# Attention and experts on one Trainium2 core: the gate's terms in two products, a gather and a scatter that wait for relus, and waits of PSUM tiles one by one

## The chip, the cores and the metric

One core of one Trainium2 chip. The metric is the device time of one launch in microseconds (us), median of the runs; lower is better. TensorE is PE in the tables, VectorE DVE, ScalarE ACT, GpSimd POOL, SyncE SP.

## The reference, cut to what matters

```
def attention(q, k, v, g_q, g_k):                 # 8 x 12 x 448 x 64
    q_n, k_n = rmsnorm(q, g_q), rmsnorm(k, g_k)
    scores = q_n @ k_n.T / 8
    attn = softmax(scores)
    return attn @ v
x = attention(...).transpose(0, 2, 1, 3).reshape(3584, 768)

logits = x @ w_gate                               # 8 experts
expert_idx = argmax(logits, 1)
gate_w = softmax(logits)[arange(N), expert_idx]
out = zeros(3584, 768)
for e in range(8):
    tok = the (at most 80) tokens of expert e with the largest gate_w
    h = maximum(x[tok] @ w1[e], 0)                # 768 x 1024
    out[tok] = gate_w[tok] * (h @ w2[e])          # 1024 x 768
```

## The kernel before, in words

**Attention.** 24 groups, each a batch and four of its 12 heads (three groups to a batch). For a group, ACT and DVE normalise q and k (L307 to L344), PE transposes them (L381), ACT copies the transposes (L410, L412), PE makes the scores (`ps`, L423), ACT exponentiates them (`at`, L426), DVE sums them over the keys (`sm`, L456, L458) and PE multiplies with v (`po`, L440). The softmax is not divided here: the rows `xb` stay undivided, are copied by ACT (L743) and stored to DRAM (`xr_scratch`) beside the reciprocals `rz` of their sums; a row is divided when an expert takes it up.

**Gate.** Once a batch, PE makes the gate's products per head and the sums (`zl`, L475), which come back transposed as `zs` (the last batch: `zt`). `gate1v` (L510) has two reciprocals of the sums (L516, one for each pair of heads `u`) and four products (L524, one for each head of a group of four), term by reciprocal, into `lx`; `gate2` (L538) reduces `lx` over the 12 heads to the logits `lg` (L541), finds the largest, and ACT exponentiates and casts (L553, L555). Behind this come the merge steps that keep, batch by batch, the best 80 tokens of each expert (`mp`, `row`, L624 to L720). All of it is put between the groups' matmuls in an order written out by hand. The last batch's gate and merge are done apart (L930 to L1146), where `by_head`, `by_block` and `by_half` divide that batch's rows with `rz`, and `xno` the rows gathered as `xo`.

**Experts.** A loop over e = 0 to 7 (L1181). In each turn PE makes `ph` from the transposed rows `xgT` and w1 (L1188, two PSUM tiles of 24 matmuls), ACT casts them through two relus into `h_sb` (L1192), DVE divides the next expert's gathered rows in three pieces of four heads (`normal(e + 1)`, L1157, `xg` into `xn`), PE transposes these (`xpose`, L1172, `pxt`), DVE copies them to `xgT` (L1174), PE multiplies `h_sb` with w2 (`py`, L1219), and DVE weights the product (`yo`, L1224). PE takes these in that order, expert by expert. Rows come in by an indirect DMA on POOL's queue (`gather`, L1119) and go out by another (`scatter`, L1209). The first gather is issued before the loop (L1123); `gather(2)` and `gather(3)` follow it at L1180, so that POOL has three issues in a row; the later ones, `gather(e + 4, wait=True)`, wait for a memset on DVE (L1118) and are issued in the loop. A gather brings 80 rows of 780 floats. The second expert's turn (e = 1) has no `normal` of its own, since `normal(2)` is done at the end of e = 0. The last expert is scattered in two halves (`idxL`), the others whole (`idxT`).

**Weights.** Weights of later experts are staged in DRAM and fetched on SP's queue as buffers come free (`fetch_late`, L242, 1,536 KB each; `fetch_part`, L928, the second part of one w2, which waits for a memset at L927 that `normal(1)` issues behind its first piece).

PSUM tiles of the experts' part come from the pool `moe_ps` (L1150), which takes over the space of the pools that were closed before it.

Of the kernel before, what the change touches and what calls it, by code (L numbers as in the profile page):

```python
# [21 lines left out]
def kernel(  # L22
# [243 lines left out]
    with av_stack:  # L266
# [243 lines left out]
        def gate1v(b):  # L510
            zt = gst[b]["zt"]
            NT = NJ + 1
            ztv = zt.rearrange("p r (j c) -> p r j c", c=64)
            rz = gpool.tile([128, NT, H], F32, tag="rz", name="rz")
            for u in range(2):
                nc.vector.reciprocal(  # L516
                    rz[:].rearrange("p j (i u hh) -> p j u i hh", u=2, hh=2)[:, :, u],
                    ztv[:, 1 - u].rearrange("p j (hh r) -> p j r hh", hh=2)[
                        :, :, 24:24 + NQ])
            lx = gpool.tile([128, NT, E, H], F32, tag="lx", name="lx", bufs=1)  # L520
            for u in range(2):
                for hh in range(2):
                    r = 32 * u
                    nc.vector.tensor_mul(  # L524
                        lx[:].rearrange("p j e (i k) -> p j k i e", k=4)[:, :, 2 * u + hh],
                        ztv[:, hh, :, r:r + NQ * E].rearrange("p j (i e) -> p j i e", e=E),
                        rz[:].rearrange("p j (i k) -> p j k i", k=4)[:, :, 2 * u + hh]
                        .unsqueeze(3).to_broadcast([128, NT, NQ, E]))
            gst[b]["lx"] = lx
            gst[b]["rz"] = rz  # L530
            rows = xr_dram[b * S:(b + 1) * S, DM:XW].rearrange("(p x) h -> p x h", x=NX)
            for t in range(2):
                n = NJ + 1 - t if b < B - 1 else NJ
                nc.sync.dma_start(out=rows[:, t:t + 2 * n - 1:2], in_=rz[64 * t:64 * t + 64, :n])
            if b == B - 1:
                nc.sync.dma_start(out=rows[:, NX - 1], in_=rz[64:, NJ])

        def gate2(b):  # L538
            NT = NJ + 1
            lg = gpool.tile([128, NT, E], F32, tag="lg", name="lg")  # L540
            nc.vector.reduce_sum(out=lg[:], in_=gst[b]["lx"][:], axis=AX.X)  # L541
            lmax = gpool.tile([128, NT], F32, tag="lmax", name="lmax")
# [390 lines left out]
    m, NT = gst[b], NJ + 1  # L933
    xbs, rz = [st[NQ * b + i]["xb"] for i in range(NQ)], m["rz"]
    xbn = [mpool.tile([128, NT, 256], BF16, tag="yo", name="xbn", bufs=3) for _ in range(NQ)]

    def by_head(i, part):
        for n in part:
# [3 lines left out]
                                 xbs[i][:, j, h * D:h * D + D], AF.Copy,  # L942
                                 scale=rz[:, j, 4 * i + h:4 * i + h + 1])

    def by_block(i, j):
        nc.vector.tensor_mul(
            xbn[i][:, j].rearrange("p (hh u d) -> p u hh d", hh=2, u=2),
            xbs[i][:, j].rearrange("p (u hh d) -> p u hh d", u=2, hh=2),
            rz[:, j, 4 * i:4 * i + 4].rearrange("p (u hh) -> p u hh", hh=2)
            .unsqueeze(3).to_broadcast([128, 2, 2, D]))  # L950

    def by_half(i, u, eng=nc.vector):
        eng.tensor_mul(
            xbn[i][:].rearrange("p j (hh u d) -> p u j hh d", hh=2, u=2)[:, u],
            xbs[i][:].rearrange("p j (u hh d) -> p u j hh d", u=2, hh=2)[:, u],
            rz[:, :, 4 * i + 2 * u:4 * i + 2 * u + 2].unsqueeze(3).to_broadcast([128, NT, 2, D]))

# [51 lines left out]
    def rows_normal(i, xn, xg):  # L1009
        c = slice(256 * i, 256 * i + 256)  # L1010
        return (xn[:, c].rearrange("p (hh u d) -> p u hh d", hh=2, u=2),
                xg[:, c].rearrange("p (u hh d) -> p u hh d", hh=2, u=2),
                xg[:, DM + 4 * i:DM + 4 * i + 4].rearrange("p (u hh) -> p u hh", hh=2)
                .unsqueeze(3).to_broadcast([CAP, 2, 2, D]))

    for h in range(4):
        u, hh = divmod(h, 2)
        o = hh * 128 + u * D
        nc.scalar.activation(xno[:, o:o + D], xo[:, h * D:h * D + D], AF.Copy,
                             scale=xo[:, DM + h:DM + h + 1])  # L1020
    stay = tpool.tile([CAP, E], BF16, name="stay")
# [84 lines left out]
    xgs = {}  # L1106
    def gather(e, wait=False):

# [8 lines left out]
        if wait:  # L1117
            nc.vector.memset(xgs[e][:, 0:1], 0.0)  # L1118
        nc.gpsimd.indirect_dma_start(  # L1119
            out=xgs[e], out_offset=None, in_=xr_dram[:, :],  # L1120
# [28 lines left out]
    ps_stack.close()  # L1149
    mps = ctx.enter_context(tc.tile_pool(name="moe_ps", bufs=2, space=PSUM))  # L1150


    def normal(e, behind=None):
        xg = xgs[e]
        xn = mpool.tile([CAP, DM], BF16, tag="xn", name="xn")
        for i in range(NQ):
            nc.vector.tensor_mul(*rows_normal(i, xn, xg))  # L1157
            if behind and not i:
                behind()
        return xn  # L1160
# [17 lines left out]

    for e in range(2, 4):
        gather(e)  # L1180
    for e in range(E):  # L1181
# [12 lines left out]
        if e + 1 < E and e != 1:  # L1194
            xn = normal(e + 1, (lambda: fetch_part(slice(FE, FC), True)) if not e else None)
        if 0 < e < E - 1:
# [5 lines left out]

        def scatter(half=None):
            if half is None:
                o, at, y, n = outs[e], idxT[:, e:e + 1], yo[:, :], N
            else:
# [6 lines left out]
        pw = DN if e + 1 < E else DN // 2  # L1213
        pys = [mps.tile([CAP, pw], F32, tag=("py", "py", "pz", "pxt")[i], name="py",
                        bufs=2 if i < 2 else 1) for i in range(DM // pw)]

# [10 lines left out]
        if e + 1 < E:  # L1227
# [7 lines left out]
            for i in range(2):  # L1235
                weighted(i)
            scatter()
        else:
            for fh in range(2):
                for i in range(2):  # L1240
# [46 lines left out]
```

## Time and profile before

| | |
|---|---|
| median of 3 runs | 409.39 us (408.94 to 409.46) |
| the profiled execution | 408.7 us, its span 407.0 us |
| PE busy | 395.7 us (97%) |
| DVE busy | 352.2 us (87%) |
| ACT busy | 320.6 us (79%) |
| POOL busy | 90.2 us (22%) |
| DMA | 100.92 MB, mean 248 GB/s |
| mean granted TensorE clock | 0.999 of full speed |

The span is the time from the first to the last instruction of the profiled execution; 1.7 us of its 408.7 lie around it. A busy share is an average over stages, so the stretch in question and its waits have to be looked at apart. In a row of the timeline the first number is the start, the second the duration, and the brackets tell how long the engine stood idle before and what ended that.

### The profile page before, as it was taken

The numbers are of one execution on the slowest core, as the hardware profiler recorded it, in microseconds if no ns is written. First come the engines' busy times: TensorE is split into PE (matmuls) and PEld (weight loads), VectorE is DVE, ScalarE is ACT, GpSimd is POOL, SyncE is SP. The second block draws the span as 40 slices with busy tenths as digits, with TensorE's granted clock in tenths as the row PEclk, the third lists the DMA queues.
The fourth block names the chain that finished last, engine by engine and source line by source line (L and its number), as shares of the span: only waits on it lengthen the run. The fifth ranks groups of instructions, "written<-read, shape, count | busy, mean of one in ns | idle before, by whom it ended". The sixth has DMA issues, their size and how long they took to land.

```text
span 407.0 us, 12628 instructions
## 1 busy us (share of the span) xinstructions
PE 395.7 (97%) x5285; PEld 195.4 (48%) x5285; DVE 352.2 (87%) x658; ACT 320.6 (79%) x508; POOL 90.2 (22%) x150
## 2 busy tenths in 40 slices
PE   8999999999999999999999999999999999999994
PEld 7334444444444444444444444444443453458884
DVE  5899987998999999997999999979999968876552
ACT  6899979997989889988899799979897877572110
POOL 7200002501031012220251024020512020154322
PEclk9999999999999999999999999999999999999999
DMA  7459999999989999989999999999999759798991
GB/s 244 144 159 212 272 296 257 273 217 304 254 223 264 246 260 263 294 205 228 243 306 217 243 278 230 289 237 285 219 205 297 161 195 374 245 277 274 342 333 52
DMA packets 76105, 100.92 MB, mean 248 GB/s; under 512 B 8448, under 2 KB 65280, under 8 KB 76048
## 3 DMA queue, kind: packets, MB, share of 16 engines
q1 hardware_dynamic: 60176, 70.99, 54.7%
q0 software_dynamic: 15872, 29.13, 39.3%
q8 instruction: 41, 0.67, 0.6%
q14 instruction: 16, 0.13, 0.1%
HBM read 101.11 MB, written 39.89 MB: 346 GB/s over the span
## 4 chain that ended last, share of the span: by engine, by line
PE 73%; DVE 12%; ACT 8%; issue 5%; POOL 2%; POOLq 0%; DVEq 0%
PE ps L423 26%; PE po L440 25%; PE zl L475 5%; DVE sm L458 4%; PE tp L381 4%; PE xp L381 3%; DVE ms L314 2%; DVE qn L344 2%; PE py L1219 2%; PE wps L894 2%; ACT at L426 1%; PE ph L1188 1%; POOL out_dram L1209 1%; ACT qkT L412 1%; PE mp L666 1%
## 5 line engine op out<-in xcount | busy, mean ns | idle before, releaser
L426 ACT ACTIVATE at<-ps 128x896 f32<-128x896 f32 x168 | 146.5, 930 | 4.5 <-PE ps L423 3.9
L423 PE MATMUL ps<-qkT 64*64 64x448 f32 x1344 | 147.3, 548 | 2.5 <-ACT row L624 1.3
L440 PE MATMUL po<-at,vt 64*64 64x448 f32 x1344 | 142.5, 537 | 0.0
L458 DVE TENSOR_TENSOR sm<-sm,at 128x896 f32<-128x896 f32 x120 | 130.7, 1089 | 3.4 <-ACT at L426 0.5
L440 PEld LDWEIGHTS po<-at,vt 64*64 64x64 f32 x1344 | 50.1, 133 | 74.0 <-issue 63.9
L423 PEld LDWEIGHTS ps<-qkT 64*64 64x64 f32 x1344 | 43.8, 132 | 66.6 <-issue 26.2
L314 DVE TENSOR_REDUCE ms<-sq 128x14 f32<-128x896 f32 (+1 forms) x50 | 52.1, 1043 | 6.9 <-ACT sq L307 6.8
L344 DVE TENSOR_TENSOR qn<-qk,rs 128x896 f32<-128x896 f32 (+1 forms) x47 | 50.5, 1077 | 1.3
L307 ACT ACTIVATE sq<-qk 128x896 f32<-128x896 f32 (+1 forms) x48 | 44.7, 930 | 2.0 <-DMA qk<-in_q_dram 1.1
L229 POOL COPY mark<-mark 1x1 bf16<-1x1 bf16 x22 | 7.8, 354 | 138.0 <-DVE mark L228 138.0
L743 ACT COPY xb<-xp 128x1024 f32<-128x1024 f32 x24 | 24.3, 1011 | 8.4 <-PE xp L381 8.3
L381 PEld LDWEIGHTS tp<-ident,qn 64*128 64x128 f32 x672 | 23.5, 139 | 12.1 <-issue 6.0
L381 PE MATMUL tp<-ident,qn 64*128 64x64 f32 x672 | 27.2, 226 | 0.3 <-DVE qn L344 0.3
L1192 ACT ACTIVATE h_sb<-ph 128x320 bf16<-128x320 f32 x16 | 7.0, 438 | 25.7 <-PE ph L1188 25.7
L447 ACT COPY us<-po 128x896 f32<-128x896 f32 (+1 forms) x24 | 21.4, 894 | 6.5 <-PE po L440 6.4
L456 DVE TENSOR_TENSOR sm<-at 128x896 f32<-128x896 f32 x24 | 26.0, 1084 | 0.1
L412 ACT COPY qkT<-tp 128x896 f32<-128x896 f32 x24 | 22.0, 917 | 3.3 <-PE tp L381 3.1
L410 ACT ACTIVATE qkT<-tp,gqk 128x896 f32<-128x896 f32 x23 | 23.6, 1025 | 0.0
L1219 PE MATMUL py<-w_sb,h_sb 128*80 128x384 bf16 (+1 forms) x144 | 22.4, 309 | 0.0
L475 PE MATMUL zl<-us,wgs 64*32 64x448 f32 x192 | 20.3, 540 | 0.0
L1224 DVE TENSOR_SCALAR yo<-py,gwT 80x384 f32<-80x384 f32 (+1 forms) x18 | 10.0, 568 | 11.7 <-PE py L1219 11.6
L475 PE MATMUL zl<-sm,zsel 64*32 64x448 f32 x192 | 20.1, 541 | 0.0
(202 smaller groups left out, 433.2 us busy)
## 6 DMA issues: line engine op xcount, KB each, us to landing
wb_scratch<-in_moe_w_dram POOLq DMA_DIRECT2D x20, 768.0 KB, 10.5
w_sb<-wb_scratch SPq DMA_DIRECT2D x8, 1536.0 KB, 11.4
vt<-in_v_dram SPq DMA_DIRECT2D x24, 448.0 KB, 7.6
out_dram<-zeros SPq DMA_DIRECT2D x28, 384.0 KB, 10.0
qk<-in_q_dram SPq DMA_DIRECT2D x23, 448.0 KB, 6.5
qk<-in_k_dram SPq DMA_DIRECT2D x23, 448.0 KB, 5.3
w_sb<-in_moe_w_dram POOLq DMA_DIRECT2D x6, 1536.0 KB, 14.9
xr_scratch<-xb SPq DMA_DIRECT2D x48, 192.0 KB, 6.7
```

The source lines that it names most:

```text
L307: nc.scalar.activation(o, x, AF.Square)
L314: nc.vector.reduce_sum(out=st[g]["ms"][:, a, lo:hi], in_=st[g]["sq%d" % a][:, lo:hi], axis=AX.X)
L344: e.tensor_mul(qn[:].rearrange("p (x hh) d -> p hh x d", hh=2)[:, h0:h1], qk[:, lo:hi].rearrange("p (hh x) d -> p hh x d", x=NX), rs[:, lo ...
L381: nc.tensor.transpose(o, w, one[p, p], tile_position=(p.start, 0))
L412: nc.scalar.copy(T[:], tp[:, :, :S])
L423: nc.tensor.matmul(ps[u * 64:u * 64 + 64, hh, :S], T1[d, u, x * 64:(x + 1) * 64], T0[d, u, :], start=True, stop=True)
L426: nc.scalar.activation(at[:], ps[:, :, :S], AF.Exp)
L440: nc.tensor.matmul(po[u][hh * D:(hh + 1) * D, u, :S], vt[p, hh * NX + x, :], at[p, hh, :], start=(x == 0), stop=(x == RD - 1))
L456: nc.vector.tensor_add(s["sm"][:], s["at0"][:], s["at1"][:])
L458: nc.vector.tensor_add(s["sm"][:], s["sm"][:], s["at%d" % x][:])
L475: nc.tensor.matmul(t[32 * c:32 * c + 32, r, :S], w, x, start=(i == 0), stop=(i == NQ - 1))
L1219: nc.tensor.matmul(pys[i][:, :], h_sb[:, fc, :], chunk(e, 1, fc)[:, i * pw:i * pw + pw], start=(fc == 0), stop=(fc == FC - 1))
```

## The change

It has four parts.

1. `gate1v` makes one reciprocal of 48 columns and two products of 192 columns; the products are taken by half (`hh`), over both `u` at once, with the heads innermost in `lx`. The reduction to `lg` goes over two axes. `rz` has another order of its 12 columns, and every reader of it follows.
2. The pool `moe_ps` is opened with `reuse_waits="tile"`: a tile waits for what lay in its own place, no longer the pool for all. The `py` tiles of expert 0 are allocated ahead of the loop.
3. `gather(3)` leaves the row of issues ahead of the loop. `normal(1)` issues it behind its second piece, after a cast on DVE of one element of `h_sb`, written by the second relu of expert 0, into the gather's tile.
4. The scatter of expert 6 is issued in the turn of expert 7, after a copy on DVE of one element of that turn's `h_sb` and a copy of the scatter's indices (`at6`), ahead of the products.

```diff
@@ gate1v
-            for u in range(2):
-                nc.vector.reciprocal(
-                    rz[:].rearrange("p j (i u hh) -> p j u i hh", u=2, hh=2)[:, :, u],
-                    ztv[:, 1 - u].rearrange("p j (hh r) -> p j r hh", hh=2)[
-                        :, :, 24:24 + NQ])
-            lx = gpool.tile([128, NT, E, H], F32, tag="lx", name="lx", bufs=1)
-            for u in range(2):
-                for hh in range(2):
-                    r = 32 * u
-                    nc.vector.tensor_mul(
-                        lx[:].rearrange("p j e (i k) -> p j k i e", k=4)[:, :, 2 * u + hh],
-                        ztv[:, hh, :, r:r + NQ * E].rearrange("p j (i e) -> p j i e", e=E),
-                        rz[:].rearrange("p j (i k) -> p j k i", k=4)[:, :, 2 * u + hh]
-                        .unsqueeze(3).to_broadcast([128, NT, NQ, E]))
+            nc.vector.reciprocal(
+                rz[:].rearrange("p j (u i hh) -> p u j i hh", u=2, hh=2),
+                ztv[:, ::-1].rearrange("p u j (hh r) -> p u j r hh", hh=2)[:, :, :, 24:24 + NQ])
+            lx = gpool.tile([128, 2 * NT, E, 2 * NQ], F32, tag="lx", name="lx", bufs=1)
+            for hh in range(2):
+                nc.vector.tensor_mul(
+                    lx[:].rearrange("p v e (i hh) -> p v i e hh", hh=2)[..., hh],
+                    zt[:, hh].rearrange("p (v r) -> p v r", r=32)[:, :, :NQ * E].rearrange(
+                        "p v (i e) -> p v i e", e=E),
+                    rz[:].rearrange("p j (u i hh) -> p (j u) i hh", u=2, hh=2)[:, :, :, hh]
+                    .unsqueeze(3).to_broadcast([128, 2 * NT, NQ, E]))
@@ gate2
-            nc.vector.reduce_sum(out=lg[:], in_=gst[b]["lx"][:], axis=AX.X)
+            nc.vector.reduce_sum(
+                out=lg[:], in_=gst[b]["lx"][:].rearrange(
+                    "p (j u) e k -> p j e u k", u=2), axis=AX.XY)
...
@@ gather
-    def gather(e, wait=False):
+    def gather(e, behind=None, wait=False):
...
         if wait:
             nc.vector.memset(xgs[e][:, 0:1], 0.0)
+        if behind is not None:
+            nc.vector.tensor_copy(xgs[e][:1, 0:1], behind)
@@ the experts' PSUM pool
-    mps = ctx.enter_context(tc.tile_pool(name="moe_ps", bufs=2, space=PSUM))
+    mps = ctx.enter_context(tc.tile_pool(name="moe_ps", bufs=2, space=PSUM, reuse_waits="tile"))
@@ normal
             nc.vector.tensor_mul(*rows_normal(i, xn, xg))
-            if behind and not i:
-                behind()
+            if behind:
+                behind(i)
@@ ahead of the loop
-    for e in range(2, 4):
-        gather(e)
+    def sums(pw):
+        return [mps.tile([CAP, pw], F32, tag=("py", "py", "pz", "pxt")[i], name="py",
+                         bufs=2 if i < 2 else 1) for i in range(DM // pw)]
+
+    pys = sums(DM // 2)
+    gather(2)
+
+    def second(i):
+        if i == 0:
+            fetch_part(slice(FE, FC), True)
+        elif i == 1:
+            gather(3, h_sb[:1, FC - 1, 0:1])
@@ in the loop
-            xn = normal(e + 1, (lambda: fetch_part(slice(FE, FC), True)) if not e else None)
+            xn = normal(e + 1, None if e else second)
...
-            scatter()
+            if e + 2 < E:
+                scatter()
+            else:
+                last = scatter
         else:
+            nc.vector.tensor_copy(mark[:, :1], h_sb[:1, FC - 1, 0:1])
+            at6 = mpool.tile([CAP, 1], U32, name="at6", bufs=1)
+            nc.vector.tensor_copy(at6[:, :], idxT[:, e - 1:e])
+            last(at=at6)
```

How instructions move, at three places. First DVE around the taking up of expert 1's rows (`xn` is divided from `xg`; the memset of `w_sb` releases the held fetch, that of `xg` the fifth gather). Before, then with the change:

```order
L1145 CAST xgT<-xT 128x240
L1157 TENSOR_TENSOR xn<-xg 80x2x2x64
L927 MEMSET w_sb 128x1
L1157 TENSOR_TENSOR xn<-xg 80x2x2x64 x2
L1118 MEMSET xg 80x1
L1145 COPY xgT<-pxt 128x240
```

```order
L1146 CAST xgT<-xT 128x240
L1158 TENSOR_TENSOR xn<-xg 80x2x2x64
L926 MEMSET w_sb 128x1
L1158 TENSOR_TENSOR xn<-xg 80x2x2x64
L1119 CAST xg<-h_sb 1x1
L1158 TENSOR_TENSOR xn<-xg 80x2x2x64
L1117 MEMSET xg 80x1
L1146 COPY xgT<-pxt 128x240
```

A cast has come between the second and third piece; the fourth gather on POOL waits for it. On POOL the order of the issues is the same as before.

Second PE at the start of the experts, with the semaphores that each waits for (`hot` are matmuls without a use, `w_sb` is w1 of expert 0). Before, then with the change:

```order
L601 MATMUL hot<-tri,identb 128x512
L1188 LDWEIGHTS w_sb [waits DVE_49,PE_49,DMASW2_49]
L1188 MATMUL ph<-xgT,w_sb 128x80 [waits Activation_49]
L1188 LDWEIGHTS w_sb
L1188 MATMUL ph<-xgT,w_sb 128x80
L1188 LDWEIGHTS w_sb
L1188 MATMUL ph<-xgT,w_sb 128x80
L1188 LDWEIGHTS w_sb
L1188 MATMUL ph<-xgT,w_sb 128x80
```

```order
L600 MATMUL hot<-tri,identb 128x512
L1200 LDWEIGHTS w_sb [waits DVE_49,DMASW2_49]
L1200 MATMUL ph<-xgT,w_sb 128x80 [waits Activation_49]
L1200 LDWEIGHTS w_sb
L1200 MATMUL ph<-xgT,w_sb 128x80
L1200 LDWEIGHTS w_sb
L1200 MATMUL ph<-xgT,w_sb 128x80
L1200 LDWEIGHTS w_sb
L1200 MATMUL ph<-xgT,w_sb 128x80 [waits DVE_49]
```

The wait for DVE's half of `xgT` has gone from the first weights to the fourth matmul; the DVE wait that is left at the first weights is an earlier one.

Third DVE at the end, from the last expert's transposes on. Before, then with the change:

```order
L1174 COPY xgT<-pxt 128x480 [waits DVE_49,PE_49]
L1224 TENSOR_SCALAR yo<-py,gwT 80x384 [waits DMASW7_49,PE_49]
L1224 TENSOR_SCALAR yo<-py,gwT 80x384 [waits PE_49]
L1224 TENSOR_SCALAR yo<-py,gwT 80x192 [waits DMASW0_49,DVE_49,PE_49]
L1224 TENSOR_SCALAR yo<-py,gwT 80x192 [waits PE_49] x3
```

```order
L1175 COPY xgT<-pxt 128x480 [waits DVE_49,PE_49]
L1236 TENSOR_SCALAR yo<-py,gwT 80x384 [waits DMASW7_49,PE_49]
L1236 TENSOR_SCALAR yo<-py,gwT 80x384 [waits PE_49]
L1254 COPY mark<-h_sb 1x1 [waits Activation_49]
L1256 COPY at_6531<-idxT 80x1
L1236 TENSOR_SCALAR yo<-py,gwT 80x192 [waits DMASW0_49,DVE_49,PE_49]
L1236 TENSOR_SCALAR yo<-py,gwT 80x192 [waits PE_49] x3
```

Two copies have come between the products of expert 6 and those of expert 7; the seventh scatter waits for them.

## Rows read from the trace of the kernel before

**Rows 1.** Page, part 1: busy time, share of the span and instructions of each engine.

```profile
PE 395.7 (97%) x5285; PEld 195.4 (48%) x5285; DVE 352.2 (87%) x658; ACT 320.6 (79%) x508; POOL 90.2 (22%) x150
```

**Rows 2.** Stretches: length, busy us (instructions) by engine, granted clock, DMA share, GB/s.

```profile
376.00:402.00 26.00, 25.51 (x380) 21.40 (x376) 13.90 (x33) 4.75 (x11) 8.17 (x9) 1.00 0.85 280
402.00:404.00 2.00, 0.00 (x0) 0.00 (x0) 0.00 (x0) 0.00 (x0) 0.92 (x1) 1.00 0.21 61
```

**Rows 3.** Waits of PE, 20 to 350 us: us in total, times, longest us.

```profile
PE ps L423 <- ACT row L624: 1.3, 3, 0.4
PE mp L381 <- ACT at L426: 0.6, 3, 0.2
```

**Rows 4.** Chain of waits, 94 to 124 us: start us, us, what.

```profile
110.72 0.37 DVE rz L516 x2
111.09 0.72 DVE lx L524 x4
```

**Rows 5.** DVE's groups by shape: busy us, mean ns of one, idle before.

```profile
L456 DVE TENSOR_TENSOR sm<-at 128x896 f32<-128x896 f32 x24 | 26.0, 1084 | 0.1
...
L524 DVE TENSOR_TENSOR lx<-zs,rz 128x96 f32<-128x96 f32 x28 | 5.7, 322 | 0.0
```

**Rows 6.** Timeline of PE, 354 to 380 us: start us, us, what, idle before.

```profile
364.93 1.88 PE L1188 MATMUL ph<-xgT,w_sb 128*128 128x80 bf16 x48 [0.16 <-DVE xgT L1145]
...
375.73 0.40 PE L1172 MATMUL pxt<-identb,xn 80*128 80x80 bf16 x6
```

**Rows 7.** Timeline of DVE, 362 to 377 us.

```profile
366.88 0.77 DVE L1157 TENSOR_TENSOR xn<-xg 80x256 bf16<-80x256 f32 x2 [2.10 <-DMA xg<-xr_scratch,idxG]
...
367.57 0.41 DVE L1157 TENSOR_TENSOR xn<-xg 80x256 bf16<-80x256 f32 x1
367.93 0.06 DVE L1118 MEMSET xg<- 80x1 f32 x1
...
374.75 1.08 DVE L1157 TENSOR_TENSOR xn<-xg 80x256 bf16<-80x256 f32 x3
```

**Rows 8.** Timeline of ACT, 360 to 408 us.

```profile
366.85 0.44 ACT L1192 ACTIVATE h_sb<-ph 128x320 bf16<-128x320 f32 x1 [0.42 <-PE ph L1188]
...
398.85 0.44 ACT L1192 ACTIVATE h_sb<-ph 128x320 bf16<-128x320 f32 x1 [0.36 <-PE ph L1188]
```

**Rows 9.** Timeline of POOL, 354 to 408 us.

```profile
365.49 0.91 POOL L1119 DMA_INDIRECT xg<-xr_scratch,idxG  x1 [0.30 <-issue]
368.28 0.91 POOL L1119 DMA_INDIRECT xg<-xr_scratch,idxG  x1 [1.88 <-DVE xg L1118]
...
398.02 0.91 POOL L1209 DMA_INDIRECT out_dram<-yo,idxT  x1 [3.71 <-DVE yo L1224]
400.92 0.91 POOL L1209 DMA_INDIRECT out_dram<-yo,idxL  x1 [1.99 <-DVE yo L1224]
402.91 0.92 POOL L1209 DMA_INDIRECT out_dram<-yo,idxL  x1 [1.08 <-DVE yo L1224]
```

**Rows 10.** The tile xg: time from a gather's issue to its landing.

```profile
DMA to landing us min/median/max: 3.8/7.3/9.2
```

**Rows 11.** DMA issues, 368 to 369 us: what, KB, us to landing.

```profile
w_sb<-wb_scratch SPq DMA_DIRECT2D x1, 1536.0 KB, 11.4
xg<-xr_scratch,idxG POOLq DMA_INDIRECT x1, 9.2
```

**Rows 12.** DMA queues, 369.3 to 372.5 us: packets, MB, share of 16 engines.

```profile
q1 hardware_dynamic: 573, 1.04, 97.1%
```

**Rows 13.** DMA queues, 372.5 to 377.6 us.

```profile
q0 software_dynamic: 96, 0.41, 24.0%
```

**Rows 14.** DMA queues and issues, 356 to 357 us.

```profile
q1 hardware_dynamic: 318, 0.39, 106.1%
...
xo<-xr_scratch,idxO POOLq DMA_INDIRECT x1, 4.7
```

**Rows 15.** Timeline of DVE, 396 to 408 us.

```profile
401.55 0.41 DVE L1224 TENSOR_SCALAR yo<-py,gwT 80x192 f32<-80x192 f32 x1 [0.25 <-PE py L1219]
```

More of the change, by code (lines that the diff above doesn't have):

```diff
@@ L933 @@
     m, NT = gst[b], NJ + 1
-    xbs, rz = [st[NQ * b + i]["xb"] for i in range(NQ)], m["rz"]
+    xbs = [st[NQ * b + i]["xb"] for i in range(NQ)]
+    rz = m["rz"][:].rearrange("p j (u i hh) -> p j u i hh", u=2, hh=2)
     xbn = [mpool.tile([128, NT, 256], BF16, tag="yo", name="xbn", bufs=3) for _ in range(NQ)]
@@ L942, in by_head @@
                                  xbs[i][:, j, h * D:h * D + D], AF.Copy,
-                                 scale=rz[:, j, 4 * i + h:4 * i + h + 1])
+                                 scale=rz[:, j, u, i, hh:hh + 1])
     def by_block(i, j):
@@ L948, in by_block @@
             xbs[i][:, j].rearrange("p (u hh d) -> p u hh d", u=2, hh=2),
-            rz[:, j, 4 * i:4 * i + 4].rearrange("p (u hh) -> p u hh", hh=2)
-            .unsqueeze(3).to_broadcast([128, 2, 2, D]))
+            rz[:, j, :, i].unsqueeze(3).to_broadcast([128, 2, 2, D]))
     def by_half(i, u, eng=nc.vector):
@@ L955, in by_half @@
             xbs[i][:].rearrange("p j (u hh d) -> p u j hh d", u=2, hh=2)[:, u],
-            rz[:, :, 4 * i + 2 * u:4 * i + 2 * u + 2].unsqueeze(3).to_broadcast([128, NT, 2, D]))
+            rz[:, :, u, i].unsqueeze(3).to_broadcast([128, NT, 2, D]))
     by_half(2, 0, nc.gpsimd)
@@ L1012, in rows_normal @@
                 xg[:, c].rearrange("p (u hh d) -> p u hh d", hh=2, u=2),
-                xg[:, DM + 4 * i:DM + 4 * i + 4].rearrange("p (u hh) -> p u hh", hh=2)
+                xg[:, DM:DM + H].rearrange("p (u i hh) -> p u i hh", u=2, hh=2)[:, :, i]
                 .unsqueeze(3).to_broadcast([CAP, 2, 2, D]))
@@ L1019 @@
         nc.scalar.activation(xno[:, o:o + D], xo[:, h * D:h * D + D], AF.Copy,
-                             scale=xo[:, DM + h:DM + h + 1])
+                             scale=xo[:, DM + u * (H // 2) + hh:DM + u * (H // 2) + hh + 1])
     stay = tpool.tile([CAP, E], BF16, name="stay")
@@ L1201, with scatter @@
         yo = mpool.tile([CAP, DM], F32, tag="yo", name="yo", bufs=3)
-        def scatter(half=None):
+        def scatter(half=None, at=None, e=e, yo=yo):
             if half is None:
-                o, at, y, n = outs[e], idxT[:, e:e + 1], yo[:, :], N
+                o, at, y, n = outs[e], idxT[:, e:e + 1] if at is None else at[:, :], yo[:, :], N
             else:
@@ L1213 @@
         pw = DN if e + 1 < E else DN // 2
-        pys = [mps.tile([CAP, pw], F32, tag=("py", "py", "pz", "pxt")[i], name="py",
-                        bufs=2 if i < 2 else 1) for i in range(DM // pw)]
+        if e:
+            pys = sums(pw)
         def product(i, fcs):
```

## The prediction, made before the changed kernel ran

> **What bounds the kernel now.** I read the busy shares first. TensorE (PE) is busy 97% of the span [rows 1], so time is won only where PE stands idle, and lost wherever it is made to. The stretches come next: from 376 to 402 us PE has 25.51 of 26 us filled, and the missing half microsecond is about what lies behind its last matmul (VectorE takes up the last product at 401.55 [rows 15]); the granted clock is 1.00, which is the full level of 2.4 GHz; in the 2 us after 402, with no matmul at all, the clock still reads 1.00 [rows 2]. A short idle of PE therefore costs its own length here and no slower clock behind it. PE's waits in the attention part are few: it waits for ScalarE (ACT) three times each at two places, 1.3 and 0.6 us in total [rows 3], the two places within one batch each time. The chain of waits that leads to such a pair runs back through ACT to VectorE (DVE), which works there without a pause and has the gate's reciprocals and products on its list [rows 4]. The timelines of the experts' part then show for each step how late its input may come.
>
> **The gate's terms.** The change takes two reciprocals (24 columns) and four products (96) per batch and makes one reciprocal (48) and two products (192). The elements stay; three fixed starts go. The four products take 0.72 us of the chain, 0.18 each [rows 4]. 800 columns more make a product 1084 - 322 = 762 ns longer, 0.95 ns a column; 1084 ns over all 896 columns is 1.21 [rows 5]. Two products of 192 columns so take 2 x (0.18 + 96 x 0.95 to 1.21 ns) = 0.54 to 0.59, and 0.13 to 0.18 is saved. I take 0.13. For the reciprocals I take nothing off 0.37: the first product now waits for the whole of one, where the second overlapped the first. The reduction reads the same 384 columns in another order; I cost it at nothing. A DVE saving passes through ACT to both of PE's waits in three batches: 3 x 0.13 = **0.39 us less**. The other batches have no such wait, so PE's own matmuls hide what they save. Ends: 0.4 more (if the longer strides cost a product what its start saved) and 1.1 less (half of the reciprocals' 0.37 also gone: 0.18 + 0.18 each). In the last batch the same saving is worth between 0 and 0.13; ACT has head products queued ahead of the exponential that reads it, so I take 0.
>
> **The first expert.** PE's first ph matmul follows an idle of 0.16 us that VectorE's half of xgT ended [rows 6]. Now the first three matmuls wait only for ACT's half and the fourth for VectorE's, so those three fill that idle: 0.16 less for PE, between 0 and 0.16. The end gets it only if nothing later waits for something else.
>
> **The fourth gather.** This decides. Before, GpSimd (POOL) issued it at 365.49, as the third of three in a row [rows 9]. The seven gathers take 3.8 to 9.2 us to land [rows 10]; even with the longest it would be down at 374.69, before VectorE takes it up at 374.75 [rows 7]. After the change it is released by a one-element cast on VectorE that waits for the second relu. That relu ends at 366.85 + 0.44 = 367.29 [rows 8]; VectorE is still at the second of three pieces of xn (first pair from 366.88, third from 367.57) and reaches the cast at 367.57 [rows 7]. The cast itself is as short as the memset of 0.06 [rows 7]; it delays the third piece by that much, which PE, still at expert 0's py, does not see, and would cost 0.06 if it did. POOL started a gather 0.35 after such a memset (367.93 to 368.28) [rows 7, 9], so this one starts at 367.92, 2.43 us later than before.
>
> Those 2.43 us move it on POOL past nothing, but past two issues of SP: the held part of w2 and the w1 of expert 6. The old fifth gather, issued at 368.28, took 9.2 us to land, next to that w1, a fetch of 1,536 KB [rows 11]. The reason stands in the queues: from 369.3 to 372.5 SP's queue q1 held 97.1% of the 16 engines and POOL's q0 moved not one packet [rows 12]; only after 372.5 did q0 get 24.0% [rows 13]. Our gather is issued 0.36 before that one, behind the same fetches. Taken with its 9.2 it lands at 367.92 + 9.2 = 377.12, which VectorE's xn of expert 3 must wait for: 377.12 - 374.75 = 2.37 late. PE began that expert's transposes at 375.73 [rows 6], with the last piece of xn ready at 374.75 + 1.08 = 375.83, so at most 0.1 of that is slack: **2.27 us more**. Behind the waiting xn on VectorE stand the cast of xgT and expert 2's yo, and PE's py of expert 2 stands behind the transposes, so PE has nothing to fill the hole with. The hole also swallows the first expert's 0.16. The fifth gather follows 0.91 + 0.30 behind [rows 9], at 369.13, and with the same 9.2 lands at 378.33; its xn comes after expert 3's xn (now to 378.2) and ph (1.88 [rows 6]), so it and those after it stay covered.
>
> Ends of the landing: 4.7 us, as the gather xo took amid a full q1 [rows 14], would be 372.6 and in time (0 more); the median 7.3 [rows 10] gives 375.2, 0.37 more; 9.2 gives the 2.27. I take 9.2, since that gather is the one with the same neighbours, 0.36 us away.
>
> The Trainium skill speaks against this ("DMA: Bandwidth & Descriptors", "Queues, rings and completion order"): each engine takes turns between the queues that have work, a packet at a time. By that rule a gather waits for one packet of the fetch, not for the fetch, and the sum would have no 2.27. The trace is divided: xo at 4.7 agrees, the 3.2 us without any q0 packet do not.
>
> **The seventh scatter.** It was issued at 398.02, and now waits for the last relu, 398.85 + 0.44 = 399.29 [rows 8, 9]. Two short copies on VectorE follow it, before yo is due, so it starts about 399.8 and takes 0.91; the next scatter, before at 400.92, starts some 0.30 after it, at 401.0: 0.1 late, or 0.4 if the copies take 0.3 more. The last scatter starts only at 402.91 [rows 9] and so hides that: nothing. Below and above see the rivals.
>
> **The sum.** 2.27 - 0.39 = 1.88 more. The profiled execution took 408.7 us (span 407.0) and would take 410.6; the median of the three runs, 409.39, is 0.7 higher, and 1.88 on it gives **411.3 us**. For this case I give 410.3 (landing 8.2, halfway from 7.3 to 9.2: 1.3 - 0.39) to 412.0 (9.2, the gate's terms 0.4 dearer).
>
> **Rivals.**
> (a) Not slower: the engines' turns. The gather is posted 0.36 us before the old fifth one; if it still gets its turn ahead of the large fetch, it lands in time. The point that decides: landing before 367.92 + 7.3 = 375.2 costs less than the gate gives. In time the sum is -0.39 - 0.16 = -0.55: **408.8**. For it speaks xo's 4.7 [rows 14], against it the 9.2 and the empty q0 [rows 11, 12].
> (b) Faster: (a) and a shorter tail. The last scatter started at 402.91, though its yo ended at 401.55 + 0.41 = 401.96 [rows 9, 15]: 0.95 between them, where the gather of 368.28 followed the end of its memset (367.99) by 0.3 [rows 7, 9]. If the extra 0.65 comes from the seventh scatter's place and goes with it, the sum is -1.2: **408.2**. Against it: the seventh is moved nearer, not away. Turned round, if the two last keep their 1.99 apart (400.92 to 402.91), the delay of the first, up to 0.4, reaches the end: 411.7 with the main case, 409.2 with (a).
> (c) The change doesn't do what it says: the wait would bind nothing if the relu were over before the old issue. It is not (367.29 against 365.49), so I give this no chance of its own.
>
> **How the numbers follow.** A measurement of this kernel tells about 0.2%, 0.82 us, from no change: 408.57 to 410.21. Main case 0.73: slower by more than that if the landing takes over 8.1 us (0.63), else within it (0.10). (a) 0.17: within 0.13, faster 0.04, when the gate gives more than I took. (b) 0.10: faster 0.09, within 0.01. Together faster 0.13, same 0.24, slower 0.63. The range goes from 408.5, which leaves out (b) and a little of (a), some 0.12, to 412.0, above which I put 0.05.
>
> **What would show it.** Right: POOL's third gather row at about 367.9; DVE's xn of expert 3 with an idle of some 2 us ended by the DMA into xg; an equal idle of PE before the pxt of expert 3; PE's waits for ACT in three batches each shorter by about 0.1; no idle before the first ph matmul; the seventh scatter at about 399.8 and the last near 402.9 plus the shift. Wrong: a landing of that gather under 7.3 us (then (a) or (b)), or a new wait of PE at any other expert.

## The result

| | before | with the change |
|---|---|---|
| median | 409.16 us (408.39 to 409.76, 8 runs) | 411.95 us (410.10 to 413.70, 8 runs) |
| ratio | | 1.0067, 95% interval 1.0042 to 1.0092 |
| profiled execution, its span | 408.7 us, 407.0 us | 410.39 us, 408.7 us |

The change makes the kernel slower by 0.67%, and its runs spread over 3.6 us where those of the kernel before spread over 1.4. The profiled execution is the second shortest of the eight, so its rows show a small form of the loss; a second profile, further down, shows a large one.

The fourth gather first. The DMA issues from 368 to 369 us of the changed kernel (what, KB, us to landing):

```profile
xg<-xr_scratch,idxG POOLq DMA_INDIRECT x1, 7.9
```

Its issue on POOL, and the first and the last of the tail's three scatters (start us, us, what, idle before):

```profile
368.39 0.91 POOL L1120 DMA_INDIRECT xg<-xr_scratch,idxG  x1 [2.92 <-DVE xg L1119]
...
401.46 0.91 POOL L1221 DMA_INDIRECT out_dram<-yo,at  x1 [5.49 <-DVE at L1256]
...
404.57 0.92 POOL L1221 DMA_INDIRECT out_dram<-yo,idxL  x1 [0.98 <-DVE yo L1236]
```

DVE around it (same columns), first the gate of one batch, then the experts:

```profile
110.43 0.44 DVE L515 RECIPROCAL rz<-zs 128x48 f32<-128x48 f32 x1
110.91 0.86 DVE L520 TENSOR_TENSOR lx<-zs,rz 128x192 f32<-128x192 f32 x2
111.61 1.09 DVE L458 TENSOR_TENSOR sm<-sm,at 128x896 f32<-128x896 f32 x1
```

```profile
367.30 0.77 DVE L1158 TENSOR_TENSOR xn<-xg 80x256 bf16<-80x256 f32 x2 [2.23 <-DMA xg<-xr_scratch,idxG]
...
367.98 0.13 DVE L1119 CAST xg<-h_sb 1x1 f32<-1x1 bf16 x1
...
376.39 1.09 DVE L1158 TENSOR_TENSOR xn<-xg 80x256 bf16<-80x256 f32 x3 [1.49 <-DMA xg<-xr_scratch,idxG]
```

PE at experts 0, 2 and 3:

```profile
364.96 1.93 PE L1200 MATMUL ph<-xgT,w_sb 128*128 128x80 bf16 x48
...
374.09 1.88 PE L1200 MATMUL ph<-xgT,w_sb 128*128 128x80 bf16 x48
376.87 0.92 PE L1173 MATMUL pxt<-identb,xn 80*128 80x80 bf16 x6 [0.90 <-DVE xn L1158]
377.62 2.77 PE L1231 MATMUL py<-w_sb,h_sb 128*80 128x384 bf16 x16
```

The gather that was issued at 365.49 [rows 9] is issued at 368.39 and lands 7.9 us later; DVE's xn of expert 3, which started at 374.75 without a wait [rows 7], stands idle for 1.49 us until the DMA lands and starts at 376.39; and PE, which went from ph to pxt without a gap [rows 6], stands idle for 0.90 us and then waits for the pieces of xn one by one (pxt takes 0.92 instead of 0.40). From the start of expert 2's ph to that of its py are 377.62 - 374.09 = 3.53 us. Without the hole it is 1.96 us (a second profile of the kernel before, below), so the hole costs 1.57.

What PE waits for from 20 to 410 us (us in total, times, longest):

```profile
PE mp L381 <- ACT at L426: 1.0, 3, 0.3
PE pxt L1173 <- DVE xn L1158: 0.9, 1, 0.9
PE pse L967 <- DVE eqb L573: 0.5, 1, 0.5
```

Against [rows 3], the wait for the batches' mp has grown from 0.6 to 1.0 instead of shrinking, and the wait for eqb (in the last batch's gate) is 0.5, against 0.3 in the second profile of the kernel before:

```profile
PE pse L968 <- DVE eqb L574: 0.3, 1, 0.3
```

DVE's groups of the gate (busy us, mean ns of one, idle before):

```profile
L520 DVE TENSOR_TENSOR lx<-zs,rz 128x192 f32<-128x192 f32 x14 | 6.1, 517 | 0.2
...
L515 DVE RECIPROCAL rz<-zs 128x48 f32<-128x48 f32 x7 | 3.1, 444 | 0.0
```

A product of 192 columns takes 517 ns where one of 96 took 322 [rows 5], and the one reciprocal of 48 columns takes 444 ns, where one of 24 took 270. These prices and the starts of the same batch in the kernel before:

```profile
L516 DVE RECIPROCAL rz<-zs 128x24 f32<-128x24 f32 x14 | 3.2, 270 | 0.0
```

```profile
110.64 0.46 DVE L516 RECIPROCAL rz<-zs 128x24 f32<-128x24 f32 x2
...
111.66 1.08 DVE L458 TENSOR_TENSOR sm<-sm,at 128x896 f32<-128x896 f32 x1
```

In the timeline of the changed kernel, the gate of this batch holds DVE from 110.43 to the start of the next sum at 111.61, 1.18 us; in that of the kernel before the same two starts are 1.02 us apart.

### The profile page after: what moved, and what is told of

It is laid out like the page before. It is cut to its first block, busy times and chain, and to the rows that moved or that the text cites. A ratio compares the mean times of both kernels' runs of the same rounds, so it can differ in the third digit from the quotient of the medians.

```text
span 408.7 us, 12608 instructions
## 1 busy us (share of the span) xinstructions
PE 395.9 (97%) x5285; PEld 195.3 (48%) x5285; DVE 353.9 (87%) x637; ACT 320.2 (78%) x508; POOL 90.2 (22%) x150
## 5 line engine op out<-in xcount | busy, mean ns | idle before, releaser
L381 PEld LDWEIGHTS xp<-ident,us 64*128 64x128 f32 x384 | 14.0, 139 | 12.0 <-ACT at L426 10.6
```

The lines of the kernel that those rows point to most:

```text
L381: nc.tensor.transpose(o, w, one[p, p], tile_position=(p.start, 0))
```

## The experiments

Each kernel ran beside the kernel before, on the same chip; e1 to e4 together, e5 to e8 together, e9 to e12 together. The kernel before had a median of 410.46, 409.45 and 409.12 us in the three groups. Comparisons are made within a group. The ratios and their intervals are those on record; they need not be the quotients of the two medians (in e11 the medians are equal and the ratio is 0.9989).

### e1: the fourth gather back in its old place

```diff
     gather(2)
+    gather(3)
...
         if i == 0:
             fetch_part(slice(FE, FC), True)
-        elif i == 1:
-            gather(3, h_sb[:1, FC - 1, 0:1])
```

> The changed kernel with the fourth gather issued ahead of the loop again, without its wait; the gate's terms, the tiles and the seventh scatter stay changed. Theory A (the late gather makes the loss): the xn of expert 3 no longer waits for a landing, PE's hole of about 1.6 us ahead of expert 2's py is gone, and the time falls from 412.0 to about 409.4, which is the old 409.2 plus some 0.45 for the gate's terms (three batches and the last) less some 0.2 for the first expert; the spread of the runs falls back to that of the kernel before (1.4 us instead of 3.6). Theory B (the loss comes from the gate's terms and the seventh scatter, and the wait for the gather only takes the place of another): still 411 to 412.

Measured: 411.3 us (410.35 to 412.22) against 410.46; ratio 1.0031 (1.0019 to 1.0043). The hole ahead of expert 2's py is gone, and the spread is back to 1.9 us. But the time is 0.84 above the kernel before, not 0.25 (the gate's waits explain 0.47 of it; the rest is open, the more so as the moved scatter spares this kernel a loss at expert 7, told in the last section), and a new wait has come. ACT's relus of expert 0 in e1:

```profile
367.61 0.77 ACT L1203 ACTIVATE h_sb<-ph 128x320 bf16<-128x320 f32 x2 [2.44 <-PE ph L1199]
```

PE there, and the gather's issue on POOL beside them:

```profile
365.22 1.93 PE L1199 MATMUL ph<-xgT,w_sb 128*128 128x80 bf16 x48
368.10 2.14 PE L1230 MATMUL py<-w_sb,h_sb 128*80 128x384 bf16 x12 [0.95 <-ACT h_sb L1203]
```

```profile
366.03 0.91 POOL L1120 DMA_INDIRECT xg<-xr_scratch,idxG  x1 [0.30 <-issue]
```

The first relu reads the first half of ph, 24 of 48 matmuls that take 1.93 us from 365.22; in [rows 8] the second relu starts 1.92 us after the start of ph, with its end. Here both start late: the first at 367.61, 2.39 after the start of ph, and PE waits 0.95 us for it. POOL is issuing the fourth gather at the time (366.03, for 0.91 us). So neither theory had it whole: the late gather makes the hole, as A says, but its old place has a cost of its own in this group of runs, which the first profile of the kernel before did not show.

### e2: the fourth gather's wait alone

The kernel before, with this part of the change and no other:

```diff
...
-    for e in range(2, 4):
-        gather(e)
+    gather(2)
+    def second(i):
+        if i == 0:
+            fetch_part(slice(FE, FC), True)
+        elif i == 1:
+            gather(3, h_sb[:1, FC - 1, 0:1])
```

> The kernel before with the wait of the fourth gather alone. Theory A: 1.6 to 4 us more than before, 411 to 412.5, with the wide spread of the changed kernel; the gather lands 7.5 to 9.5 us after its issue, and DVE's xn of expert 3 waits for it. Theory B: within 0.4 us of before, since the wait only matters with the other parts.

Measured: 411.6 us (410.98 to 414.38) against 410.46; ratio 1.0031 (1.0019 to 1.0044), with the wide spread. Its profile is of the longest of its seven runs (414.38). PE's waits in it:

```profile
PE pxt L1174 <- DVE xn L1159: 1.6, 1, 1.6
...
PE py L1227 <- ACT h_sb L1200: 0.4, 1, 0.4
```

Its py of expert 2:

```profile
379.40 4.45 PE L1227 MATMUL py<-w_sb,h_sb 128*80 128x384 bf16 x16
```

The hole is here too (1.6 us ahead of the first piece), py behind it takes 4.45 us where it takes 2.77 in both profiles of the kernel before (e6 below shows why), and the relus of expert 0 are on time: the only wait for h_sb is one of 0.4 at the end. So the wait for the relus does what the edit says where POOL's issue would have held them, and loses more by the gather than it wins.

### e3 and e10: the gate's terms alone

The kernel before with part 1 of the change (the first two hunks of its diff, and the readers of rz).

> The kernel before with the gate's terms alone. Theory A (one reciprocal of 48 columns holds the first product back, and products of 192 columns cost twice those of 96): gate1v takes 1.18 us instead of 1.02, PE waits about 0.1 longer in three batches and 0.16 longer for the last batch's eqb: 0.4 to 0.5 more, 409.6. Theory B (as forecast, the saved starts are worth 0.13 in three batches): 0.4 less, 408.8.

> The kernel before with the gate's terms alone, once more. Theory A (gate1v longer by 0.16): 0.4 to 0.5 us slower than before on any chip, hold or not, since its waits lie ahead of the experts. Theory B (forecast): 0.4 faster.

Measured: 410.72 against 410.46, ratio 1.0011 (0.9993 to 1.0029); again in the third group 410.47 (409.18 to 412.84) against 409.12, ratio 1.0023 (0.9999 to 1.0048). Neither interval is clear of no change by itself; the gain that was forecast, 0.39 us or a ratio of 0.9990, lies outside both. The waits of PE in e10:

```profile
PE mp L381 <- ACT at L426: 0.9, 3, 0.3
PE pse L967 <- DVE eqb L573: 0.5, 1, 0.5
```

They are those of the changed kernel, 0.3 and 0.2 above the kernel before. The waits tell what the times alone do not: in all seven profiles of kernels with these terms they are 0.9 to 1.0 and 0.5, in all seven without them 0.6 to 0.7 and 0.3. What the runs of e10 that took up to 412.8 us spent beyond this isn't in any profile; on record the mean granted clock is 0.992 to 0.995 in the three longest and 0.996 to 0.998 in the other nine.

### e4 and e9: the waits of the PSUM tiles alone

```diff
-    mps = ctx.enter_context(tc.tile_pool(name="moe_ps", bufs=2, space=PSUM))
+    mps = ctx.enter_context(tc.tile_pool(name="moe_ps", bufs=2, space=PSUM, reuse_waits="tile"))
...
+    pys = sums(DM // 2)
...
-        pys = [mps.tile(...)]
+        if e:
+            pys = sums(pw)
```

> The kernel before with the waits of the PSUM tiles one by one alone. Theory A (three matmuls start ahead of DVE's half of xgT, and PE is continuous from there to the end): 0.15 to 0.25 less, 409.0, and no idle of PE ahead of the first ph. Theory B (something later gives it back): no difference.

> The kernel before with the waits of the PSUM tiles alone, once more. In its first run the relus of expert 0 were held until POOL had issued the fourth gather, so an earlier ph won nothing (PE waited 0.94 us for h_sb, with the gate's terms alone 0.72). Theory A: on a chip without the hold it is 0.15 to 0.25 us faster than before; with the hold there is no difference again. Theory B (no gain at all): no difference on either.

Measured: 410.22 against 410.46, ratio 0.9998 (0.9989 to 1.0007); again 408.90 against 409.12, ratio 0.9995 (0.9973 to 1.0016). PE's idle ahead of the first ph is gone in both. In e4 PE then waited for the held relus:

```profile
PE py L1224 <- ACT h_sb L1197: 1.4, 2, 0.9
```

That is 0.94 us at expert 0 and 0.44 at expert 7, where e3 had 0.72 at expert 0: what ph won was lost at the relu. In the third group no relu was held, and the median is 0.22 lower than that of before; the interval can't tell that from nothing. Inconclusive by time, as expected by the rows.

### e5 and e6: the two kernels again

> The kernel before, unchanged, for a second profile of it. Where the fourth gather keeps its old place, three profiles have shown expert 0's two relus held back until about 1.4 us after the start of POOL's issue (starting 1.1 to 1.3 us after the ph that they read), and PE waiting 0.7 to 0.95 us for them; the first profile of the kernel before showed neither. Theory A (the hold is a matter of the chip or the execution, not of the kernels): the hold shows here too on the chip of those runs, with PE's wait for h_sb, and the time is about 1.3 us above 409.2; on another chip it may be absent. Theory B (the edits of those kernels brought the hold): absent here, and the time is near 409.2.

> The changed kernel, unchanged, on the same chip as the kernel before again. Theory A: no relu of expert 0 and none of expert 7 is held, since POOL issues nothing beside them (0.95 and 0.45 us of PE's waits gone where the chip shows the hold), the fourth gather lands 7 to 9.5 us after its issue and PE waits 1.5 to 3.5 us for xn of expert 3; the sum is about 1 us more than before where the hold shows, and 2.5 more where it doesn't. Theory B (the relus are as before): 2.5 more on any chip.

The kernel before: 409.17 against 409.45, ratio 0.9994 (0.9984 to 1.0005). No relu was held. The changed kernel: 414.2 us (413.75 to 415.01, four runs), ratio 1.0124 (1.0109 to 1.0139). That is more than theory A's 2.5, and its profile shows why. The gather in e6 (time from issue to landing), and PE in e5 and then in e6 from expert 2 on:

```profile
DMA to landing us min/median/max: 3.6/7.4/9.6
```

```profile
374.58 1.88 PE L1188 MATMUL ph<-xgT,w_sb 128*128 128x80 bf16 x48
...
376.54 2.77 PE L1219 MATMUL py<-w_sb,h_sb 128*80 128x384 bf16 x16
```

```profile
373.86 1.88 PE L1200 MATMUL ph<-xgT,w_sb 128*128 128x80 bf16 x48
378.64 0.92 PE L1173 MATMUL pxt<-identb,xn 80*128 80x80 bf16 x6 [2.90 <-DVE xn L1158]
379.39 4.17 PE L1231 MATMUL py<-w_sb,h_sb 128*80 128x384 bf16 x16
383.35 2.19 PE L1200 MATMUL ph<-xgT,w_sb 128*128 128x80 bf16 x48
```

The gather took 9.6 us, and PE's idle is 2.90 us before the transposes; from ph to py are 379.39 - 373.86 = 5.53 us against 376.54 - 374.58 = 1.96, a hole of 3.57. And then py takes 4.17 us instead of 2.77, and the next ph 2.19 instead of 1.88: another 1.71. The stretches of e6 (length, busy us of PE, PEld, DVE, ACT and POOL, granted clock, DMA share, GB/s) say what that is:

```profile
380.00:381.00 1.00, 1.00 (x7) 0.67 (x5) 0.06 (x2) 0.00 (x0) 0.65 (x1) 0.79 1.03 353
...
383.00:384.00 1.00, 1.00 (x12) 0.79 (x11) 0.41 (x2) 0.00 (x0) 0.00 (x0) 0.50 1.08 375
384.00:385.00 1.00, 1.00 (x32) 1.00 (x30) 1.00 (x4) 0.22 (x1) 0.51 (x1) 1.00 1.07 387
```

The granted clock fell to 0.50, which is the lower level of 1.2 GHz, about two microseconds after PE had begun to work again, and came back at 384. In the first profile of the changed kernel, with an idle of 0.90, it stayed at 1.00 until the last matmul; in e2, with 1.60, it fell too. So the two profiles show a loss of about 1.6 us where the gather is not very late, and of about 5.3 (3.57 + 1.71) where it is, and the median of 411.95 lies between. On record the mean granted clock is 0.993 in the two longest of the result's eight runs (413.47 and 413.70) and 0.996 or 0.997 in the six others (410.10 to 412.88), and 0.989 to 0.995 in the four of e6. So the clock seems to have fallen in two of the eight, and the others to differ by the length of the hole; all but one of them (410.39) were not profiled, so this is argued and not shown. A hole of this gather is not the only thing that goes with such runs: the kernel before has five of 35 at 0.993 or 0.994 in the third group (410.89 to 412.00), and no profile tells why.

### e7: the large fetch sent behind the gather

The changed kernel; SP's fetch of expert 6's w1 now waits for a memset that DVE reaches ahead of expert 2's xn:

```diff
             if not e:
+                load_weights(wpool, NW0 + 3, 0)
+                nc.vector.memset(w_tiles[NW0 + 3][0][0][:, 0, 0:2], 0.0)
                 xn = normal(2)
...
-            load_weights(wpool, NW0 + 3 + e, e)
+            if e:
+                load_weights(wpool, NW0 + 3 + e, e)
```

> The changed kernel with SP's fetch of expert 6's w1 held by a memset on DVE that stands ahead of expert 2's xn, so that it is sent about 1.5 us later, behind the fourth gather. Theory A (the gather waits in the DMA engines for that large fetch): it now lands 4 to 5.5 us after its issue, DVE's xn of expert 3 and PE do not wait for it, and the time is 1.5 to 3 us below the changed kernel's. Theory B (any gather that is issued so late takes long, whatever lies ahead of it): 7 to 9 us as in the changed kernel, and no gain.

Measured: 410.37 us (409.56 to 411.71), ratio 1.0028 (1.0016 to 1.0041), where the changed kernel had 1.0124 beside it. The issues from 367.5 to 369.2 us of e7, SP's issues, DVE's xn of expert 3, and PE's py at the last expert:

```profile
w_sb<-wb_scratch SPq DMA_DIRECT2D x1, 384.0 KB, 3.2
xg<-xr_scratch,idxG POOLq DMA_INDIRECT x1, 5.9
```

```profile
370.46 9.01 SPq L242 DMA_DIRECT2D w_sb<-wb_scratch  x4
```

```profile
375.81 1.08 DVE L1158 TENSOR_TENSOR xn<-xg 80x256 bf16<-80x256 f32 x3
```

```profile
400.41 2.81 PE L1231 MATMUL py<-w_sb,h_sb 128*80 128x192 bf16 x32 [0.58 <-ACT h_sb L1204]
```

The same gather, issued as late, now lands in 5.9 us, with the smaller fetch (384 KB) still ahead of it and the large one behind; xn starts without a wait and PE has no hole. That settles that the gather waits for the large fetches; SP's next one comes later here too, so the run doesn't tell the two apart. DVE's work beside the issue is not the cause: it is the same in both kernels (expert 2's xn, then yo), and in e7 the gathers' queue q0 moves its first packets in the half microsecond from 370.5, during that xn. Theory A's 4 to 5.5 us were a little low, and so was its gain of 1.5 to 3: it is 3.8 us beside e6, which ran with the large form of the loss. What is left over the kernel before, 0.9 us, has two rows: the gate's terms, and a wait of 0.58 us at expert 7, which the profile puts down to a relu; the first products read only the first relu, which had ended at 399.50, and what PE's queue waited for there is the semaphore of the last of SP's fetches, expert 7's w2, sent at about 377.6 and landing 22.7 us later, at about 400.3. The second relu ends at 400.30 too, which is why the row names a relu. SP's row of 370.46 stands at 368.34 in e6: the fetch was held by 2.1 us, and those behind it came later too.

### e8: the gather behind the first piece

```diff
         if i == 0:
+            gather(3, h_sb[:1, 0, 0:1])
             fetch_part(slice(FE, FC), True)
-        elif i == 1:
-            gather(3, h_sb[:1, FC - 1, 0:1])
```

> The changed kernel with the fourth gather behind the first piece of expert 1's xn instead of the second, waiting for the first relu only: issued about 0.35 us earlier, ahead of SP's fetch of expert 6's w1 instead of beside it. Theory A (the order against that fetch decides): it lands in under 6 us, and the time is 1.5 to 3 us below the changed kernel's. Theory B (the traffic as a whole decides): it lands 0.35 us earlier than in the changed kernel, and the time falls by that much at most.

Measured: 410.89 us (409.13 to 413.24), ratio 1.0032 (1.0010 to 1.0054). The issues of e8 from 368 to 369 us, POOL's row, SP's row (its first is the large fetch) and DVE's xn of expert 3:

```profile
xg<-xr_scratch,idxG POOLq DMA_INDIRECT x1, 7.8
```

```profile
368.30 1.20 POOL L1120 DMA_INDIRECT xg<-xr_scratch,idxG  x1 [2.42 <-DVE w_sb L926]
```

```profile
368.61 9.17 SPq L242 DMA_DIRECT2D w_sb<-wb_scratch  x4
```

```profile
376.22 1.09 DVE L1158 TENSOR_TENSOR xn<-xg 80x256 bf16<-80x256 f32 x3 [0.90 <-DMA xg<-xr_scratch,idxG]
```

The gather was issued at 368.30, 0.31 us ahead of the large fetch, and still took 7.8 us; DVE waited 0.90 us for it. To be issued ahead of the fetch is not enough. By its packets it was not ahead: POOL's issue lasts to 369.50 here; in e7 the first packets of q0 move 1.5 to 2.0 us after the start of the issue (369.04, then none before 370.5), which would be 369.8 to 370.3 here; and from 370 to 370.5 SP's queue q1 already takes 105.4% of the engines, with nothing of q0 from 369 to 372.5. Theory B is right about the landing; the time fell by more than it allowed (411 beside 414), as its profile has a hole of 0.3 us ahead of the first piece and the clock at 1.00 throughout. A fetch sent 0.31 us behind the gather (e8) delays it, then, and one sent 1.42 us behind (e7: 369.04 and 370.46) does not.

### e11 and e12: the seventh scatter alone, and with the tiles

```diff
...
-            scatter()
+            if e + 2 < E:
+                scatter()
+            else:
+                last = scatter
         else:
+            nc.vector.tensor_copy(mark[:, :1], h_sb[:1, FC - 1, 0:1])
+            at6 = mpool.tile([CAP, 1], U32, name="at6", bufs=1)
+            nc.vector.tensor_copy(at6[:, :], idxT[:, e - 1:e])
+            last(at=at6)
```

> The kernel before with the wait of the seventh scatter alone. Theory A: where no hold shows, no difference (the scatter starts at about 399.8 to 400 and the two last follow as before); where it shows, the second relu of expert 7 is no longer held and 0.4 to 0.5 us are won. Theory B (its delay reaches the last scatter): 0.1 to 0.4 slower without the hold.

> The kernel before with the tiles and the seventh scatter of the change, without its gate's terms and with the fourth gather in its old place. Theory A: 0.2 us faster than before without the hold, 0.4 to 0.5 with it, and so the best of the kernels. Theory B: no difference.

Measured: e11 409.12 against 409.12, ratio 0.9989 (0.9969 to 1.0009); e12 408.80 (408.28 to 409.83) against 409.12, ratio 0.9984 (0.9965 to 1.0004). No relu was held in this group, so what the scatter's wait is worth with the hold was not measured by time. POOL's last rows in e12:

```profile
399.84 0.91 POOL L1221 DMA_INDIRECT out_dram<-yo,at  x1 [5.49 <-DVE at L1256]
401.06 0.91 POOL L1221 DMA_INDIRECT out_dram<-yo,idxL  x1 [0.30 <-DVE yo L1236]
402.95 0.92 POOL L1221 DMA_INDIRECT out_dram<-yo,idxL  x1 [0.98 <-DVE yo L1236]
```

The seventh scatter starts at 399.84, the first half of the last follows 0.30 behind its end, and the second half keeps 1.89 us from that, as it kept 1.99 [rows 9]. From the start of expert 7's py to that last issue are 402.91 - 398.65 = 4.26 us in the first profile of the kernel before, and 404.57 - 400.31 = 4.26 in that of the changed kernel: the delay is hidden. e12 has the lowest median of all kernels here, but its interval includes no change, so that it beats the kernel before is possible and not shown.

## Why the prediction was right, and where not

The forecast was 411.3 us in a range of 408.5 to 412.0; measured 411.95, just inside the upper end. The step that decided, the late landing of the fourth gather, was right. The number owes something to luck: the sum of the first profile, 1.7 us of span against 1.88 forecast, agrees because the hole was 0.70 shorter and the gate 0.86 dearer than forecast, and the median lies in the range because the runs fall between that form and one of 4.5 us, which the forecast did not have.

**The fourth gather** decided, as said. Its issue came at 368.39 and 368.43 in the two profiles where 367.92 was worked out: the first gather landed later (xn of expert 1 at 367.30, not 366.88), and POOL started 0.41 after the start of the cast, not 0.35. The landing was to take 9.2 us; it took 7.9 and 9.6. The hole was to be 2.27; it was 1.57 and 3.57. That the cause is the large fetch, the step taken from one row and an empty queue, is what e7 shows: the landing falls to 5.9 us with that fetch behind. Rival (a), the engines' turns, fell with the landing at 376.3, where it needed 375.2. The rule of the Trainium skill that stood beside it ("DMA: Bandwidth & Descriptors", "Queues, rings and completion order") is not refuted by that: from 372.5 on, q0 does move beside q1 [rows 13], as turns would have it; but the first of them came too late to help, and the rule doesn't tell when.

**The clock** is the step that failed for the large form: "a short idle of PE therefore costs its own length here and no slower clock behind it". It held for the idle of 0.90, and not for 1.60 and 2.90, where the granted clock fell to 0.50 for some three microseconds and cost 1.7. The row that I took for proof, 1.00 in the 2 us after the last matmul, shows only that the clock falls later than PE's idle begins; [rows 2] end before it does. From 405 to 407 us of the same trace, still without a matmul, the granted clock is 0.71:

```profile
405.00:407.00 2.00, 0.00 (x0) 0.00 (x0) 0.00 (x0) 0.00 (x0) 0.00 (x0) 0.71 0.01 4
```

**The gate's terms** had the wrong sign: forecast 0.39 less, found about 0.3 more in the three batches and 0.16 more in the last, 0.47 together (PE busy in 94 to 124 us 29.15 instead of 29.24, and the like in the two others; from 352 to 362 us 9.20 instead of 9.36, as the wait for eqb has grown). Two prices failed. A column of these products does not cost 0.95 to 1.21 ns, taken from plain rows of 896 columns: (517 - 322) / 96 = 2.0 ns, so two wide products last as long as four narrow ones. And one reciprocal is not priced like two that overlap: 444 ns for 48 columns against 270 for 24, and the first product waits for all of it.

**The first expert** went as forecast: no idle ahead of ph, 0.16 to 0.2, and in the changed kernel the hole swallows it. **The seventh scatter** cost nothing, as forecast. Rival (b)'s tail fell: the last scatter still starts 0.95 after its yo (403.21 + 0.41 in DVE's row, 404.57 on POOL).

The sum for the first profile by what was found: 1.57 + 0.47 - 0.2 = 1.8, against 1.7 of the spans. For the second: 3.57 + 1.71 + 0.47 - 0.2 = 5.6, against 412.0 - 407.5 = 4.5; the rest lies ahead of the gate's last batch, where e6 is about a microsecond earlier than e5 (the xo gather is issued at 356.44 against 356.96, though the gate costs it 0.47), and differs so between runs of any of the kernels.

## What to carry to other kernels

A small gather can wait for a large fetch of another queue, even one sent a little behind it: before a gather is moved, look at what the other queues send around its new place, and if the fetch is moved instead, count where it is then late. Price strided small products by rows of the same shape, not by plain rows; where back-to-back instructions already overlap, merging them may save nothing (here it did not), and a merged producer makes its consumer wait for the whole. A hole in a full TensorE can cost more than its length: read the granted clock behind the longest hole that is likely, not behind the shortest.

## What had not been expected of the hardware

**POOL's issue held ACT's relus, in one group of runs.** In e1 to e4 a relu that became due while POOL was issuing an indirect DMA started 1.4 to 1.6 us after the start of that issue (e1 above: 366.03 and 367.61): in e4 the second relu of expert 7 (POOL 399.44, relu 400.85).

```profile
399.44 0.91 POOL L1214 DMA_INDIRECT out_dram<-yo,idxT  x1 [3.38 <-DVE yo L1229]
```

```profile
400.85 0.44 ACT L1197 ACTIVATE h_sb<-ph 128x320 bf16<-128x320 f32 x1 [0.94 <-PE ph L1193]
```

```profile
398.20 0.92 POOL L1214 DMA_INDIRECT out_dram<-yo,idxT  x1 [3.71 <-DVE yo L1229]
```

```profile
399.03 0.44 ACT L1197 ACTIVATE h_sb<-ph 128x320 bf16<-128x320 f32 x1 [0.36 <-PE ph L1193]
```

The first pair of fences is e4, the second the same kernel in the third group (e9): there the relu starts 0.83 after the start of POOL's issue, before that has ended, with the end of PE's ph, 0.36 us after the one before instead of 0.94. That it is the issue that holds them is shown by e2, in the first group too: with the fourth gather's issue moved away, the relus of expert 0 start 1.05 and 1.91 us after ph, on time, and at expert 7 the wait is still there. Where it is held, PE loses 0.72 to 0.95 us at expert 0 and 0.40 to 0.44 at expert 7, and the kernel before was 1.0 to 1.3 us slower in that group than in the others, which agrees with it (it was not profiled there). This is what the two waits for relus remove, and with it they are worth something; without it they are not. What decides whether it shows is open. The edits aren't it: e4 and e9 are one kernel, as e3 and e10 are, and show it once and not the second time; and the first group and the second ran on the same chip.

**The clock's answer to a hole.** Idle of 0.90: none. Idle of 1.60 (e2) and 2.90 (e6): a granted clock of 0.50 for some three microseconds, in e2 from about 379.7 and in e6 from about 380.6, one and two microseconds after the work had begun again at 378.65 and 378.64. Three profiles don't show from which length on it falls, or whether the length alone decides.
